# Attention and a gated convolution in one kernel: whole-unit copies of the transposed probabilities, more extra products at the start, and another order table

## The chip, the cores and the metric

The kernel runs on one core of one Trainium2 chip. The metric is the device time of one execution in microseconds (us). A core has five instruction streams that run side by side and wait for one another through semaphores: PE (TensorE: matrix products, with the loading of weights shown apart as PEld), DVE (VectorE), ACT (ScalarE), POOL (GpSimd) and SP, whose queue (SPq) issues all the loads and stores here. Each stream works through its own list in order.

## The reference

q, k and v have 4 batches, 8 heads, 768 rows and 64 columns. Every row attends to its neighbours within 15 positions and, beside them, to one summary of each block of 32 rows (the elementwise maximum of k, the mean of v). The result, 768 x 512 a batch, goes through a gated layer.

```python
k_sum = k.reshape(B, H, nb, 32, D).max(axis=3)
v_sum = v.reshape(B, H, nb, 32, D).mean(axis=3)
scores_l = np.where(abs(i - j) < 16, q @ k.T / 8, -1e9)
scores_s = q @ k_sum.T / 8 + log(32)
a = softmax(concat[scores_l, scores_s])
x = a @ concat[v, v_sum]                     # heads side by side: B, S, 512
gate = sigmoid(causal depthwise convolution of x, 5 taps)
out = (gate * (x @ w_val)) @ w_out
```

## The kernel before

The 768 rows of a batch are cut into three thirds of 256 rows, which gives 12 groups g (4 batches by 3). Each group has two units, u = 2g and 2g + 1, of four heads each: 24 units for the attention, 12 groups for the two products with w_val and w_out. A unit's scores are eight blocks of 128 rows by 120 columns (window, own block, block summaries).

The instructions are written in the order of a table of tokens, ORDER, and each engine keeps that order. A token is a letter and its indices; a helper op_<letter> issues its instructions. Those that the text speaks of:

- PE: S.u.r scores of half a unit (two halves a unit), T.u transposes of a unit's probabilities (16 products with the identity), X.u probabilities times v, V.g.c half of x times w_val, O.g.s half of the product with w_out, VB sums of v for batch 0, VS transposes of the block sums of later batches, pw.k extra products of zeros that nothing reads.
- DVE: ks block maxima of k, N.u.c adds the mask and finds the row minimum, R.u reciprocal of the row sums, A.u.k one of the eight taps of the convolution on half a unit, gf gate times value, and the bit work on the weights (wvd, wve for w_val; wod, woe for w_out).
- ACT: E.u.c exponentials, C copies the transposed probabilities from PSUM to SBUF, H and F copy a unit's x out of PSUM (rounded and exact), I.u.r first tap, G.u gate, gh rounds gf, oe takes the output out of PSUM, wvs and wos rescale the weights, vb copies the block means of batch 0.
- POOL: mset fills the tile that pw reads, kc writes the maxima between the columns of k, M.u.r scales half a unit's probabilities, L and gl the low parts of x and of gf, tr sums blocks of v, wvc, wvb, woc and wob the high and low parts of the weights.
- SP: k, n, q, q0, v, w, o, m, c, i load; f.g.e.h copies the block means into v's tiles; st stores.

In group 0 V and O are single-pass float32 products; the others are split into 24 and 12 products of high and low parts. V.0 needs all four quarters of w_val; the four quarters of w_out are unpacked into the same tile wf, so woe.k can't begin before V.0.0 and V.0.1 are done with quarter k, and O.0 needs all of them.

PSUM has eight banks. psum_plan gives them out in two rings: two slots of two banks for the scores of a unit or its transposed probabilities (s), and four single banks for all else (p). A slot goes to the next tile once the last reader of the one before it has run. The tables of loads have two tiles each for q, k (by pair of heads) and v, so a load of v for group g + 2 waits for X of group g.

C.u.e in this kernel copies half e of a unit's 2 x 8 x 64 transposed probabilities, 512 columns of 120 partitions, so a unit has C.u.0 and C.u.1. Each pw token is two products of 128 x 64 by 104 columns; there are six of them, all into one bank.

Of the kernel before, what the change touches and what calls it, by code (L numbers as in the profile page):

```python
# [58 lines left out]
N.3.0 R.2 E.3.1 E.3.0 q.2 S.5.1 S.5.0 E.3.3 wve.1 E.3.2 N.5.0 M.2.1 N.5.3 N.5.2 N.5.1 S.4.1 wvc.1
S.4.0 n.0.1 VB.1 M.1.0 T.1 vb.0 vb.1 C.1.0 E.5.0 R.3 N.4.3 v.0.1 v.0.0 w.3 wvs.3 X.0 I.0.1 F.0 I.0.0  # L60
N.4.1 wvd.3 N.4.0 N.4.2 wve.3 w.2 wvd.2 C.1.1 M.3.0 wvc.0.1 v.1.1 X.1 v.1.0 A.0.0 A.0.1 A.0.2 M.3.1
A.0.3 k.1.3 wvb.0 M.2.0 T.2 wvs.2 E.5.1 wve.2 I.1.1 F.1 A.0.4 I.1.0 A.1.0 A.0.5 wvb.1 k.1.0 h.1
wvc.2.1 A.1.1 A.0.6 ks.1.3 kc.1.3 T.3 C.3.0 V.0.0 C.2.1 E.5.2 C.2.0 wvc.3.1 A.0.7 k.1.1 ks.1.1
kc.1.1 ks.1.0 wvb.3 kc.1.0 E.5.3 R.5 E.4.3 M.5.1 q.3 S.6.1 E.4.2 n.1.1 E.4.0 A.1.2 M.5.0 pw.5 G.0
N.6.3 gf.0.0 A.1.3 E.4.1 N.6.2 A.1.4 R.4 f.1.0.1 f.1.1.0 f.1.1.1 f.1.0.0 X.2 C.3.1 H.2 k.1.2 M.4.0
X.3 F.2 F.3 I.2.0 H.3 ks.1.2 I.3.0 S.6.0 N.6.0 N.6.1 v.2.1 T.5 C.5.1 C.5.0 A.1.5 v.2.0 A.3.0 A.2.0
I.3.1 S.7.1 A.1.6 A.3.1 A.1.7 A.3.2 kc.1.2 S.7.0 N.7.0 A.3.3 o.1 E.6.0 E.6.2 n.1.0 q.4 N.7.3 A.3.4
N.7.2 A.3.5 M.4.1 T.4 E.6.3 C.4.0 G.1 C.4.1 I.2.1 E.7.3 E.7.0 N.7.1 A.3.6 V.0.1 wod.1 tr.1.1 S.9.0
tr.1.0 gf.0.1 o.0 A.3.7 A.2.1 wod.0 A.2.2 wos.0 wos.1 woe.0 woe.1 G.3 f.2.0.0 f.2.0.1 o.2 E.7.2
S.8.1 wvb.2 L.3 wod.2 S.8.0 S.9.1 f.2.1.0 f.2.1.1 o.3 X.5 wod.3 wos.2 woe.2 h.2 L.2 woc.1.1 wos.3  # L70
woe.3 n.1.3 tr.1.3.1 F.5 E.6.1 H.5 E.7.1 X.4 F.4 H.4 woc.2 O.0.1 oe.0.1 O.0.0 A.2.3 R.6 M.6.0 A.2.4
N.9.0 M.6.1 A.2.5 N.8.3 A.2.6 R.7 A.2.7 I.5.0 G.2 I.5.1 I.4.0 N.8.1 N.8.0 N.9.1 n.1.2 tr.1.2 N.8.2
A.4.0 woc.0 v.3.0 k.2.2 k.2.3 N.9.2 A.4.1 A.5.0 v.4.1 E.8.0 n.2.0 oe.0.0 q.5 A.4.2 A.5.1 v.3.1 E.8.2
V.1.1 N.9.3 VS.1 A.5.2 gf.1.1 E.8.3 I.4.1 vs.1 T.6 L.4 M.7.0 M.7.1 T.7 C.6.1 wob.0 E.9.1 v.4.0 C.7.1
ks.2.3 kc.2.3 A.5.3 k.2.1 A.4.3 C.7.0 L.5 woc.3.1 wob.3 gh.1.1 A.5.4 f.3.1.0 f.3.0.0 f.3.0.1 wob.2
# [630 lines left out]
```

## Time and profile before

| | us |
|---|---|
| median of three timed runs | 241.03 (240.19 to 242.12) |
| profiled execution, whole | 242.98 |
| its span, first to last instruction | 241.2 |
| PE busy | 221.4 (92%) |
| ACT busy | 186.4 (77%) |
| DVE busy | 171.4 (71%) |
| POOL busy | 155.8 (65%) |

Busy times are unions over the span, and a matmul's end is modelled, so PE's share says that something was in it and not that it ran at its best. The span is what the rows below are read against; the profiled execution as a whole is 1.8 us longer.

### The profile page before, as it was taken

Reading aid. Unit: us, or ns where it says so; the run is one execution under the profiler, and the core shown is the slowest. Engines: PE = TensorE matmul, PEld = TensorE weight load, DVE = VectorE, ACT = ScalarE, POOL = GpSimd, SP = SyncE. Lnnn points to the kernel's source line nnn. Section 1 sums busy time; section 2 is a strip of 40 time slices with the busy share of each in tenths; the row PEclk is TensorE's granted clock in tenths of the full one; section 3 lists DMA queues with packets and bytes.
Section 4 is the critical chain, followed back from the end, with each engine's and each line's share of the span. In section 5 each row is a group of like instructions: output and inputs, shape, how many; then the busy total and the mean of one; then the engine's idle time right before and its main releaser. Section 6 shows DMA issues by size and latency. Waiting matters only on the chain.

```text
span 241.2 us, 7772 instructions
## 1 busy us (share of the span) xinstructions
PE 221.4 (92%) x2884; PEld 187.3 (78%) x2884; DVE 171.4 (71%) x683; ACT 186.4 (77%) x614; POOL 155.8 (65%) x219
## 2 busy tenths in 40 slices
...
GB/s 188 398 357 293 393 369 292 335 327 331 168 267 155 366 281 260 292 109 247 293 91 238 63 154 296 74 140 69 91 226 72 46 63 45 43 46 43 0 46 132
DMA packets 17318, 46.42 MB, mean 192 GB/s; under 512 B 2400, under 2 KB 3424, under 8 KB 17280
## 3 DMA queue, kind: packets, MB, share of 16 engines
...
q8 instruction: 23, 0.38, 0.6%
q14 instruction: 15, 0.12, 0.2%
...
## 4 chain that ended last, share of the span: by engine, by line
PE 71%; POOL 9%; DVE 6%; DMA 5%; ACT 4%; issue 3%; SPq 1%; POOLq 0%; ACTq 0%; DVEq 0%
PE val L567 26%; PE out L596 23%; PE x L513 9%; PE s L444 7%; POOL p L487 4%; PE pt L496 4%; DMA v<-vb 2%; DVE sn L460 2%; POOL vT L326 2%; DMA k<-in_kT_dram 1%; DVE wf L409 1%; POOL xl L533 1%; POOL gl L581 1%; DVE g L547 1%; ACT g L542 1%
## 5 line engine op out<-in xcount | busy, mean ns | idle before, releaser
L547 DVE SCALAR_TENSOR_TENSOR g<-xf,cwt,g 128x256 f32<-128x256 f32 x192 | 88.4, 483 | 12.4 <-ACT g L542 8.8
L474 ACT ACTIVATE p<-sn,nm 128x120 f32<-128x120 f32 x192 | 73.9, 397 | 5.9 <-DVE nm L460 3.0
L487 POOL TENSOR_TENSOR p<-p,ri 128x480 f32<-128x480 f32 x48 | 47.3, 1001 | 22.5 <-DVE ri L482 18.3
L460 DVE CUSTOM_DVE_ANT_0 sn<-s,mask 128x120 f32<-128x120 f32 x192 | 42.4, 276 | 14.7 <-PE s L444 14.3
L567 PE MATMUL val<-xh,wv 128*128 128x256 f32 x352 | 50.1, 284 | 0.0
L567 PEld LDWEIGHTS val<-xh,wv 128*128 128x128 f32 x352 | 45.3, 188 | 1.9 <-issue 0.6
L596 PE MATMUL out<-wo,gh 128*128 128x512 f32 x176 | 45.6, 401 | 0.0
L581 POOL TENSOR_TENSOR gl<-gf,gh 128x512 fp32r<-128x512 f32 x22 | 28.4, 1294 | 19.8 <-ACT gh L576 18.7
L474 ACT ACTIVATION_READ_ACCUMULATOR p<-sn,nm 128x1 f32 x192 | 38.5, 201 | 0.0
L596 PEld LDWEIGHTS out<-wo,gh 128*128 128x128 f32 x176 | 31.8, 188 | 7.4 <-ACT g L542 0.4
L533 POOL TENSOR_TENSOR xl<-xf,xh 128x512 fp32r<-128x512 f32 x22 | 28.4, 1295 | 9.2 <-ACT xf L528 6.6
L444 PE MATMUL s<-k,qbd 64*64 64x120 f32 x768 | 25.3, 279 | 6.8 <-POOL k L315 3.5
L444 PEld LDWEIGHTS s<-k,qbd 64*64 64x64 f32 x768 | 21.1, 140 | 11.0 <-POOL k L315 6.3
L326 POOL TENSOR_TENSOR vT<-vT 128x384 f32<-128x384 f32 (+3 forms) x48 | 27.2, 566 | 2.8
L513 PE MATMUL x<-pts,v 120*64 120x64 f32 x768 | 27.2, 224 | 1.9 <-DMA v<-vb 1.2
L513 PEld LDWEIGHTS x<-pts,v 120*64 120x64 f32 x768 | 25.3, 138 | 3.9 <-issue 1.8
L567 PE MATMUL val<-xl,wv 128*128 128x256 f32 x176 | 27.8, 279 | 0.0
L500 ACT COPY pts<-pt 120x512 f32<-120x512 f32 x48 | 26.7, 592 | 1.4 <-PE pt L496 1.3
L572 DVE SCALAR_TENSOR_TENSOR gf<-gt,val 128x512 f32<-128x512 f32 x24 | 16.4, 685 | 13.2 <-PE val L567 12.8
L596 PE MATMUL out<-wo,gl 128*128 128x512 f32 x88 | 24.3, 396 | 0.2 <-POOL gl L581 0.2
L567 PEld LDWEIGHTS val<-xl,wv 128*128 128x128 f32 x176 | 23.8, 188 | 0.0
L606 ACT ACTIVATE ob<-out 128x512 f32<-128x512 f32 x23 | 13.8, 599 | 11.6 <-PE out L596 7.6
...
## 6 DMA issues: line engine op xcount, KB each, us to landing
...
```

Of the source, the lines that this page charges most:

```text
L326: nc.gpsimd.tensor_tensor(dst, src[:, :, :n], src[:, :, n : 2 * n], ALU.add)
L444: nc.tensor.matmul(sp[64 * e : 64 * e + 64, h, c * KW : c * KW + KW], qbd[g % NQB][64 * h : 64 * h + 64, pr, i * QT : i * QT + QT], ktile( ...
L460: nc.vector.tensor_tensor_reduce(sn[:, n, :], tiles["s", u][:, h, c * KW : c * KW + KW], mask[:, mv, :], -1.0 / math.sqrt(D), 3.0e38, ALU.add,
L474: nc.scalar.activation(p[:, n, :], tiles["sn", u][:, n, :], AF.Exp, bias=tiles["nm", u][:, n : n + 1], scale=-1.0, accum_out=rs[:, u % NRS ...
L487: nc.gpsimd.tensor_tensor(p[:, w], p[:, w], ri[:, w].unsqueeze(2).broadcast_to([P, TPU, KW]), ALU.mult)
L500: nc.scalar.copy(pts[:, :, QT * e : QT * e + QT], tiles["pt", u][:KW, e])
L513: nc.tensor.matmul(dst, v[:KW, i, c0 : c0 + D], src, start=True, stop=g > 0)
L533: nc.gpsimd.tensor_tensor(xl[:, prs(u), :], xf(g)[:, prs(u), HALO:], tiles["xh", g][:, prs(u), :].bitcast(F32), ALU.subtract,)
L547: nc.vector.scalar_tensor_tensor(gt, xf(u // NHP)[:, pr, o : o + SG], cwt[:, pr, o : o + 1], gt, ALU.mult, ALU.add)
L567: nc.tensor.matmul(val[:, r], w, x, start=(n == 0), stop=(n == len(terms) - 1))
L581: nc.gpsimd.tensor_tensor(gl[:, cos, :], tiles["gf", g, cp], tiles["gh", g][:, cos, :].bitcast(F32), ALU.subtract)
L596: nc.tensor.matmul(po, x, w, start=(n == 0), stop=(n == len(terms) - 1))
```

## The change

Four things change. C.u is one copy of both halves, 1,024 columns over the two banks of the slot, in place of two of 512. There are twelve pw tokens, each with a PSUM tile of its own; the first has twelve products and the others two. The bank plan follows from that. And the table ORDER is another one: the same tokens otherwise, in another order on every engine. Two of the table's rows stand for it here.

```diff
-NWARM = 2
+NWARM = (12,) + (2,) * 11

 ORDER = """
-k.0.1 mset pw.0 q0.1 ks.0.1 k.0.0 ks.0.0 kc.0.1 S.0.1 pw.1 pw.2 kc.0.0 c cs q0.0 m N.0.3 E.0.3 N.0.2
...
+n.0.2 k.0.2 ks.0.2 q0.2 mset pw.6 pw.0 VB.2 pw.5 k.0.3 pw.2 pw.10 pw.1 kc.0.2 S.1.0 c q0.3 cd ks.0.3
...
-        return {"vb": [("vb", a[0])], "VS": [("vsp", a[0])], "vs": [("vsp", a[0])], "pw": [("pw", 0)]}.get(
+        return {"vb": [("vb", a[0])], "VS": [("vsp", a[0])], "vs": [("vsp", a[0])], "pw": [("pw", a[0])]}.get(
...
-        for j in range(NWARM):
+        for j in range(NWARM[k]):
...
-                ps(("pw", 0), [P, DM])[:QT, : QT + BASE], t[:, :QT], t[:, : QT + BASE],
+                ps(("pw", k), [P, DM])[:QT, : QT + BASE], t[:, :QT], t[:, : QT + BASE],
...
-    def op_C(u, e):
+    def op_C(u):
         pts = wt(("pts", u), [KW, NP, P], "pts")
-        nc.scalar.copy(pts[:, :, QT * e : QT * e + QT], tiles["pt", u][:KW, e])
+        nc.scalar.copy(pts.rearrange("p n (e q) -> p e n q", e=2), tiles["pt", u][:KW])
```

Three places show how instructions move. The lines of the changed kernel are two lower, since its table is two lines shorter. In a name the last number is a running count; before it stands, for k, the pair of heads.

PE at the start of the program, before (pw extra products, s scores, vb sums of v):

```order
L332 MATMUL pw_87<-ones 64x104 x2
L444 MATMUL s_99<-k_1_78,qbd_69 64x120 x8
L332 MATMUL pw_87<-ones 64x104 x4
L444 MATMUL s_99<-k_0_93,qbd_69 64x120 x8
L444 MATMUL s_148<-k_0_93,qbd_70 64x120 x8
L444 MATMUL s_148<-k_1_78,qbd_70 64x120 x8
L344 MATMUL vb_176<-vn_174,ones 64x512
L344 MATMUL vb_178<-vn_174,ones 64x512
L332 MATMUL pw_87<-ones 64x104 x2
```

PE at the start, now:

```order
L330 MATMUL pw_92<-ones 64x104 x2
L330 MATMUL pw_95<-ones 64x104 x12
L342 MATMUL vb_108<-vn_78,ones 64x512
L342 MATMUL vb_110<-vn_78,ones 64x512
L330 MATMUL pw_112<-ones 64x104 x2
L330 MATMUL pw_117<-ones 64x104 x2
L330 MATMUL pw_120<-ones 64x104 x2
L330 MATMUL pw_123<-ones 64x104 x2
L442 MATMUL s_128<-k_2_80,qbd_69 64x120 x8
L442 MATMUL s_128<-k_3_115,qbd_69 64x120 x8
```

The first scores now come from heads 2 and 3 (unit 1), and 20 extra products and a VB stand ahead of them, where two extra products stood before.

PE from V.0.0 (val_0 from xf and wf, the float32 product of group 0) on, before:

```order
L567 MATMUL val_0_590<-xf_241,wf 128x256 x8
L444 MATMUL s_627<-k_1_606,qbd_70 64x120 x8
L332 MATMUL pw_87<-ones 64x104 x2
L513 MATMUL x_667<-pts_599,v_485 64x64 x16
L513 MATMUL x_690<-pts_588,v_485 64x64 x16
L444 MATMUL s_627<-k_0_560,qbd_70 64x120 x8
L496 MATMUL pt_730<-ident,p_417 120x64 x16
L444 MATMUL s_755<-k_3_526,qbd_70 64x120 x8
L444 MATMUL s_755<-k_2_687,qbd_70 64x120 x8
L496 MATMUL pt_800<-ident,p_622 120x64 x16
L567 MATMUL val_1_832<-xf_241,wf 128x256 x8
```

PE from T.2 on, now:

```order
L494 MATMUL pt_581<-ident,p_360 120x64 x16
L330 MATMUL pw_598<-ones 64x104 x2
L565 MATMUL val_0_614<-xf_227,wf 128x256 x8
L565 MATMUL val_1_623<-xf_227,wf 128x256 x8
L494 MATMUL pt_641<-ident,p_213 120x64 x16
L494 MATMUL pt_668<-ident,p_465 120x64 x16
L511 MATMUL x_730<-pts_609,v_602 64x64 x16
L511 MATMUL x_749<-pts_747,v_602 64x64 x16
L442 MATMUL s_781<-k_1_658,qbd_70 64x120 x8
L442 MATMUL s_781<-k_0_726,qbd_70 64x120 x8
L442 MATMUL s_833<-k_3_358,qbd_70 64x120 x8
L442 MATMUL s_833<-k_2_558,qbd_70 64x120 x8
```

V.0.1 (val_1) has moved from behind X.2, X.3 and the scores of units 6 and 7 to right behind V.0.0, with T.3 and T.4 behind it and ahead of X.2.

DVE around the first block maxima of batch 1 (ks_3 from k_3, the token ks.1.3), before:

```order
L409 SCALAR_TENSOR_TENSOR wf<-sc_wv_547,wf 128x512
L547 SCALAR_TENSOR_TENSOR g_467<-xf_241,cwt,g_467 128x256
L547 SCALAR_TENSOR_TENSOR g_552<-xf_241,cwt,g_552 128x256
L547 SCALAR_TENSOR_TENSOR g_467<-xf_241,cwt,g_467 128x256
L547 SCALAR_TENSOR_TENSOR g_552<-xf_241,cwt,g_552 128x256
L547 SCALAR_TENSOR_TENSOR g_467<-xf_241,cwt,g_467 128x256
L302 TENSOR_REDUCE ks_3_567<-k_3_526 128x24
L547 SCALAR_TENSOR_TENSOR g_467<-xf_241,cwt,g_467 128x256
L302 TENSOR_REDUCE ks_1_608<-k_1_606 128x24
L302 TENSOR_REDUCE ks_0_612<-k_0_560 128x24
L481 TENSOR_REDUCE ri_619<-rs 128x8
L482 RECIPROCAL ri_619<-ri_619 128x8
```

DVE around ks.1.3, now:

```order
L407 SCALAR_TENSOR_TENSOR wf<-sc_wv_246,wf 128x512
L479 TENSOR_REDUCE ri_345<-rs 128x8
L480 RECIPROCAL ri_345<-ri_345 128x8
L458 ISA sn_332,nm_333<-s_273,mask 128x120
L458 ISA nm_333 128x1
L458 ISA sn_332,nm_333<-s_273,mask 128x120
L458 ISA nm_333 128x1
L398 TENSOR_SCALAR wf<-raw_wv_354 128x512
L300 TENSOR_REDUCE ks_3_378<-k_3_358 128x24
L407 SCALAR_TENSOR_TENSOR cwt<-sc_cw_164,cwt 128x20
L458 ISA sn_332,nm_333<-s_273,mask 128x120
L458 ISA nm_333 128x1
```

ks.1.3 stood behind most taps (g) of units 0 and 1; now it stands ahead of the last mask additions (sn) of unit 2, and so ahead of all taps.

## Rows read from the trace of the kernel before

**Rows 1.** Busy time by stage: us and instructions of PE, PEld, DVE, ACT, POOL; clock, DMA, GB/s.

```profile
0.00:73.70 73.70, 59.03 (x852) 43.53 (x852) 59.36 (x254) 59.34 (x210) 47.49 (x81) 0.98 0.86 305
...
73.70:237.10 163.40, 162.32 (x2033) 143.78 (x2032) 112.03 (x430) 126.48 (x404) 108.34 (x138) 1.00 0.44 144
```

**Rows 2.** Chain of waits, kinds of TensorE work later in the run.

```profile
73.79 1.80 PE s L444 x64
...
75.59 2.02 PE x L513 x64
...
148.88 0.43 PE vsp L360 x4
...
165.90 1.08 PE pt L496 x32
...
182.44 2.83 PE val L567 x24
...
225.95 8.40 PE out L596 x36
```

**Rows 3.** TensorE in order of time, first 65 us.

```profile
5.92 1.08 PE L444 MATMUL s<-k,qbd 64*64 64x120 f32 x16 [3.46 <-POOL k L315]
...
6.93 1.65 PE L332 MATMUL pw<-ones 128*64 128x104 f32 x8
...
14.91 1.06 PE L444 MATMUL s<-k,qbd 64*64 64x120 f32 x32
...
20.76 1.94 PE L344 MATMUL vb<-vn,ones 128*64 128x512 f32 x8
...
33.19 3.72 PE L567 MATMUL val<-xf,wf 128*128 128x256 f32 x16 [0.38 <-ACT g L542]
...
48.42 5.41 PE L567 MATMUL val<-xf,wf 128*128 128x256 f32 x16
...
57.58 7.13 PE L596 MATMUL out<-wf,gf 128*128 128x512 f32 x16
```

**Rows 4.** Chain of waits: its head by line, and one piece of it.

```profile
by line: PE val L567 26.3%; PE out L596 23.0%; PE x L513 8.5%; PE s L444 7.3%; POOL p L487 4.0%; PE pt L496 4.0%; issue 2.9%; DMA v<-vb 2.4%; DVE sn L460 2.1%; POOL vT L326 1.9%; DMA k<-in_kT_dram 1.5%; DVE wf L409 1.1%; POOL xl L533 1.1%; 
...
34.88 5.78 DMA v<-vb
```

**Rows 5.** Busy time of shorter early stretches, columns as in rows 1.

```profile
0.00:9.00 9.00, 3.80 (x32) 2.88 (x36) 2.81 (x10) 2.36 (x7) 1.70 (x14) 1.00 0.79 256
...
9.00:17.00 8.00, 7.01 (x113) 4.64 (x115) 5.12 (x32) 6.45 (x34) 1.24 (x6) 1.00 1.04 398
...
17.00:21.00 4.00, 3.47 (x46) 2.00 (x40) 3.92 (x24) 3.36 (x14) 1.64 (x2) 1.00 0.74 240
```

**Rows 6.** The same view, two later stretches.

```profile
49.40:52.60 3.20, 3.20 (x10) 2.50 (x9) 1.28 (x8) 3.20 (x13) 2.75 (x4) 0.51 0.96 296
...
60.00:112.00 52.00, 49.67 (x689) 42.01 (x689) 45.04 (x198) 48.30 (x163) 49.88 (x73) 1.00 0.71 236
```

**Rows 7.** Groups by line: three of POOL, two ACT copies out of PSUM.

```profile
L487 POOL TENSOR_TENSOR p<-p,ri 128x480 f32<-128x480 f32 x48 | 47.3, 1001 | 22.5 <-DVE ri L482 18.3 <-ACT ob L606 1.8 <-ACT p L474 1.5
...
L500 ACT COPY pts<-pt 120x512 f32<-120x512 f32 x48 | 26.7, 592 | 1.4 <-PE pt L496 1.3
...
L533 POOL TENSOR_TENSOR xl<-xf,xh 128x512 fp32r<-128x512 f32 x22 | 28.4, 1295 | 9.2 <-ACT xf L528 6.6 <-ACT xh L525 2.6
...
L326 POOL TENSOR_TENSOR vT<-vT 128x384 f32<-128x384 f32 (+3 forms) x48 | 27.2, 566 | 2.8
...
L603 ACT ACTIVATE ob<-out 128x256 f32<-128x256 f32 x1 | 0.4, 386 | 2.2 <-PE out L596 2.2
```

**Rows 8.** VectorE in order of time: its first mask addition.

```profile
7.81 0.28 DVE L460 CUSTOM_DVE_ANT_0 sn<-s,mask 128x120 f32<-128x120 f32 x1
```

**Rows 9.** All engines in order of time, the end.

```profile
236.04 1.10 PE L596 MATMUL out<-wo,gl 128*128 128x512 f32 x4
...
237.68 0.60 ACT L606 ACTIVATE ob<-out 128x512 f32<-128x512 f32 x1 [2.87 <-DMA out_dram<-ob]
```

More of the change, by code (lines that the diff above doesn't have):

```diff
@@ L59 @@
[L59 to L75, printed above, removed]
@@ new lines @@
+VB.4 k.0.0 pw.7 pw.8 N.3.0 E.3.0 N.1.1 ks.0.0 pw.3 n.0.0 VB.0 h.0 E.3.2 N.3.3 k.0.1 ks.0.1 E.1.1
+E.3.1 E.3.3 w.0 wvd.0 wvs.0 R.1 kc.0.0 q0.0 S.0.0 kc.0.1 S.0.1 S.2.1 n.0.5 S.2.0 N.0.3 n.0.1 n.0.3
+E.0.3 N.0.0 M.1.0 N.0.1 R.3 N.0.2 VB.5 i M.1.1 T.1 M.3.0 N.2.2 N.2.3 wve.0 E.0.1 E.0.0 E.0.2 R.0
+N.2.1 M.0.1 M.0.0 w.2 w.1 n.1.1 k.1.3 E.2.3 tr.1.1 VB.3 VB.1 C.1 E.2.1 wvd.1 ks.1.3 ce N.2.0 wvs.1
+wvs.2 wvd.2 pw.9 T.0 wvc.0.1 wve.2 kc.1.3 wvc.2.1 vb.0 vb.1 q.2 S.4.1 C.0 wve.1 S.4.0 N.4.1 E.2.2
+N.4.2 N.4.0 E.2.0 R.2 M.2.1 N.4.3 S.5.0 E.4.1 S.5.1 N.5.3 N.5.0 wvc.1 E.4.3 v.0.1 v.0.0 X.1 I.1.1
@@ new lines @@
+kc.2.3 wob.0 I.6.0 n.2.1 q.6 X.7 I.7.0 H.7 R.8 gf.2.0 N.10.3 N.10.1 N.11.2 st.0.0 n.2.0 F.7 A.6.0
+N.11.1 N.11.3 N.10.2 I.7.1 E.10.2 M.8.1 O.1.0 oe.1.0 f.4.1.0 M.8.0 O.1.1 M.9.0 kc.2.1 M.9.1 T.9
+N.11.0 T.8 L.6 h.4 A.6.1 A.6.2 gl.2.1 A.6.3 E.10.0 q.7 f.4.0.1 v.5.0 f.4.1.1 E.10.1 gh.2.0 k.3.0
+v.5.1 A.7.0 ks.2.2 A.7.1 A.7.2 A.6.4 E.10.3 L.7 V.3.1 E.11.2 C.8 E.11.1 C.9 gl.2.0 kc.2.2 S.13.0
+ks.2.0 kc.2.0 S.12.0 oe.1.1 E.11.0 E.11.3 A.7.3 A.6.5 R.10 M.10.0 M.10.1 S.13.1 A.6.6 A.7.4 A.7.5
+k.3.2 st.1.0 A.6.7 G.6 tr.2.0 S.12.1 f.4.0.0 X.8 A.7.6 A.7.7 G.7 N.13.3 N.13.1 E.13.1 X.9 H.8 F.8
@@ new lines @@
+N.14.3 N.14.2 F.11 A.10.0 N.14.0 N.15.2 A.10.1 A.10.2 I.11.0 n.3.2 N.15.0 gf.4.0 A.10.3 M.13.1
+A.11.0 A.11.1 N.15.1 N.15.3 E.14.1 gh.3.1 gl.3.1 E.14.0 L.10 M.13.0 V.4.1 A.10.4 gf.4.1 st.2.0
+f.7.1.1 A.11.2 st.2.1 f.6.0.1 f.6.1.0 E.14.3 gh.4.0 gh.4.1 A.11.3 A.11.4 A.11.5 E.14.2 R.14 ks.3.2
+A.10.5 A.10.6 O.3.0 T.13 C.13 A.11.6 A.11.7 A.10.7 h.6 tr.3.0 T.12 gl.4.1 L.11 C.12 E.15.0 E.15.1
+E.15.3 O.3.1 gl.4.0 S.16.1 f.7.0.1 S.17.0 S.16.0 N.16.0 oe.3.1 kc.3.0 G.11 E.15.2 S.17.1 N.16.3 G.10
+ks.3.3 M.14.1 N.17.3 f.6.0.0 N.16.2 oe.3.0 N.17.1 E.16.0 f.6.1.1 X.12 H.12 R.15 M.15.0 I.12.1 I.12.0
```

109 lines of the change are left out of this document (53 added, 56 removed).

## Prediction

> **What bounds the kernel now.** I read the busy times by stage first [rows 1]. From 73.7 us to 237.1 TensorE is busy for 162.3 of 163.4 us at the full clock; before 73.7 it is busy for 59.0, and part of that at half pace. So the second part is bound by TensorE's list, and what can be won lies in the first 73.7 us or in the list itself. To see how much, I price TensorE's list by its pieces at the full clock [rows 2]: a half of S 0.45 us (64 records, two units, 1.80), X 1.01, T 0.54, a half of V 2.83, a half of O 2.80, VS 0.43. Group 0 [rows 3]: V.0 3.5 a half (16 records in 3.72, less the tail of the last), O.0 3.5 (16 in 7.13), VB 0.95 (8 records in 1.94), X.0 and X.1, which have twice the products, 1.87. An extra product takes 0.2 us at half pace (8 records in 1.65 are four products: 0.4 each), and 0.1 a record at full pace.
>
> Up to the end of V.1.0 the old list holds 20 S, 6 VB, 8 T, 6 X, four halves of group 0, two of V.1, one VS and six pw: 48.1 us. V.1.0 ended at 73.8 (the S of [rows 2] follow it). So TensorE had **lost 25.7 us** by then. The whole list is 206.6 us and ended at 237.1 [rows 9]: 30.5 lost, so only 4.8 came after, most of it pieces a little dearer than my prices. Behind the last product come 4.1 us of copying and storing [rows 9].
>
> **The copies.** 24 copies of 1,024 columns take the place of 48 of 512 at 0.592 [rows 7]. Nearest rows: 256 columns took 0.386, so 256 more cost 0.206, and 1,024 would take 1.00, against two at 0.59 that overlap by about 0.1 when they follow one another. Bounds: 0.59 (the second bank is free) and 1.18 (it costs a full copy), so for a unit from 0.5 less to 0.1 more; I take nothing, as the slope's 1.00 is within 0.1 of the pair. ACT is not the bound after 73.7 (126.5 of 163.4), X now waits for one copy and not two. The sum doesn't hang on it.
>
> **The extra products.** 34 instead of 12. Twenty of the new ones and a VB stand ahead of the first score, and the queue of TensorE holds the score behind them. 14 products at half pace from 1.5 us on end at 7.1, VB (twice 0.95) at 9.0, 8 more at 12.2; if the clock rises after the first dozen, the first score starts at 8.7. The price is not the difference to 5.9, where the first score started [rows 3]: the mask now stands behind q.1 in the load order, 2.23 MB from the start, which is 9 to 10 us at 256 GB/s [rows 5], and the first mask addition (7.81 before [rows 8]) waits for it. Two halves of S must be through by then, at 1.08 each at half pace: 14.4 against 9.7 us. So the block costs 0 at the one end, 4.7 us at the other. Which: 16 score records at 5.92 took 1.08, 32 at 14.91 took 1.06, so the pace was 1.2 GHz until about 14, though TensorE had hardly paused from 5.9 on; the granted clock reads 1.00 there and doesn't show it. I take 1 us; the wait of ks.1.3 for its load, below, swallows it, so nothing of it enters the sum. In the Trainium skill, "TensorE: Matmul & The Clock Gate", Part 1, sustained activity releases a throttle that is the default, and the ramp is put at under 1% of a typical span, which would make the block worth less than 2.4 us either way. The trace agrees that the start is slow, and shows it lasting longer than one would read there.
>
> **The new order, TensorE's list to V.1.0.** The same count with 6 T, no VS and 8 more pw is 48.8. I follow what each piece waits for, with loads placed by their bytes in the new order. 5.5 MB were in by 17 us and 398 GB/s flowed from 9 us on; then the rate fell to 240 [rows 5], because q.2 had to wait for unit 1's scores, which came late. In the new order these scores come early and q.2 follows k.1.3, so I let the rate go on at 390 to 400.
> - DVE: the eight mask additions of units 1 and 3 run from about 9.7 without the gaps of before, then units 0 and 2. ks.1.3 stands at the head of its queue from about 21 and its load (7.3 MB) lands at about 22: 1 us or 2 lost, with the last addition of unit 2 behind it.
> - X.1 needs v.0 (8.9 MB: 26) and the copy C.0 (26): X.1 and X.0 take 26.7 to 30.4.
> - V.0.0 needs the fourth quarter of w_val (10.3 MB: 30, then rescaled and joined) and F.0: 32.3. V.0.1 follows at once, until 39.4. Before, V.0.1 started at 48.4 and took 5.4 [rows 3], as the clock had fallen to 0.51 from 49.4 to 52.6 [rows 6].
> - T.3, T.4, then X.2 at 40.6. X.2 waits for f.1, which landed at 40.7 before, after 5.8 us on the way [rows 4]. Now two loads of v.2 stand ahead of it, and these wait for X.0 (30.4); four issues of f end at 36, landing 38 to 41. So X.2 is no earlier than before, but V.0.1 and T.4 lie behind it already.
> - X.3, four S until 44.4, X.4 at 45.5. O.0.1 waits for the four quarters of w_out, unpacked one by one on ACT and DVE after X.3's copies: 48.2, so it ends at 49.5. T.5 50.0, O.0.0 53.5, X.5 54.5, four S 56.3, V.1.1 59.1, V.1.0 62.0. Before: O.0 from 57.6 on.
>
> That is 62.0 - 48.8 = 13.2 lost instead of 25.7.
>
> **Who is late next.** POOL. It worked 47.5 of the first 73.7 us, so it had lost 26.2, and 49.9 of the 52 us from 60 to 112 [rows 1, 6]: TensorE's lead can't be larger than POOL allows. The piece that decides is V.3.1, whose last products need L.7. Ahead of L.7 POOL's new list has 20 M at 0.96, 9 L and gl at 1.28, 5 tr at 2.5 [rows 7] and 22 us of weight parts and small copies: 65.4, and TensorE's list to the end of V.3.1 has 69.3. V.3.1 ends 1.7 after L.7. So TensorE's loss there is POOL's loss less 2.2. Counted as above (M.7.1, with 44.2 ahead of it, done at 61.8), POOL loses 17.6.
>
> The end follows: list 208.8 (206.6 and 22 more products at 0.1), loss at V.3.1, 4.3 for dearer pieces behind it (26.3 to 30.5 before), 4.1 of tail, so **span = 217.2 + loss at V.3.1**. POOL's counted 17.6 is a lower bound, since counting leaves out waits that the profile puts to nothing; "issue" has 2.9% of the chain [rows 4], 7.0 us. I add a third of that, 2.4, as a quarter of the span with most of the load traffic lies in question. POOL's loss 20.0, TensorE's 17.8, span 235.0. The profiled span of 241.2 stands to the median of 241.03 as -0.2, so I predict **234.8 us**.
>
> **The rivals.**
> 1. Everything goes as counted: loss 15.4, 232.4 us. For it: after 73.7 TensorE waited for nothing that cost much. Against it: before, waits without a name did occur.
> 2. POOL comes no earlier than before. ks.1.3 on DVE and tr.1.1 on POOL stand at the head of their queues before the units 2 to 5 are through, and each us that their loads land late holds all M behind them; M.11.1 now has 79.5 of POOL work ahead of it instead of 68.8. With POOL's loss at 26.2 to 26.8, TensorE's is 24 to 24.6, and the time 241.0 to 241.6: no change.
> 3. Slower: the clock. In the new list TensorE waits in small pieces between 44 and 50 (the w_out quarters, T.5 for M.5.1), as it did before the fall at 49.4 [rows 6]. If it falls there and stays at the low level through O.0, X.5 and the scores into V.1, these run at twice their price: 3.5 + 3.5 + 1.0 + 1.8 = 9.8 us, 244.6. It decides once the low level lasts some 17 us; before, it lasted 3.2.
> 4. That the change doesn't do what it says is out: the order shows one copy a unit and the twelve series.
>
> **How the numbers follow.** A measurement of this kernel tells about 1% from no change (2.4 us). Chances: forecast (232.5 to 238.5) 0.53, rival 1 with what lies below 232.5 0.16, rival 2 and the stretch up to 243.4 0.19, slower 0.12. Faster 0.69, same 0.19, slower 0.12. The range must leave out no more than 0.2: it takes in rival 1 and rival 2, 230.5 to 241.8.
>
> **What would show it.** Right: V.0.1 right behind V.0.0 before 41 us; O.0 ended before 56; V.1.0 ended at 62 to 66; POOL's idle time up to M.7.1 17 to 21 us; TensorE full from there on; one copy of about 1.0 us a unit. Wrong: the first score later than 11; f.1 landing after 44; ks.1.3 waiting more than 3 us; stretches of low clock between 40 and 60; gaps on TensorE behind 75 us, above all at V.3.1 and T.11.

## The result and the profile after

The changed kernel took **243.49 us** (median of 16, 241.69 to 246.60) beside 240.98 for the kernel before (16 runs, 238.22 to 242.81): ratio **1.0122**, 95% interval 1.0087 to 1.0157, so slower by 1.2%. The forecast was 234.8, and 243.49 lies above the whole range. (Ratios leave disturbed executions out, so they are not quite the quotient of the medians.) The profiled execution took 245.63 with a span of 243.9.

Busy time by stage of the changed kernel, cut where [rows 1] is cut (columns as there):

```profile
0.00:73.70 73.70, 62.93 (x876) 47.82 (x876) 56.29 (x240) 53.40 (x183) 46.13 (x79) 0.91 0.86 313
73.70:240.00 166.30, 164.23 (x2060) 144.18 (x2056) 117.02 (x444) 131.55 (x407) 109.59 (x141) 1.00 0.44 137
```

Behind 73.7 us TensorE is again busy nearly throughout (2.1 us idle). The first stage has a mean clock of 0.91 where it had 0.98, and its last piece, V.1.0, ends at 72.9 where 62.0 was forecast: against the forecast, that is where to look. Beside the kernel before (73.7) V.1.0 is no later, but two T and the VS, which stood ahead of it, now stand behind it. TensorE in this stage, in order of time (start, us, pieces, idle before and its releaser); the pieces of [rows 3] are among them:

```profile
8.62 2.23 PE L442 MATMUL s<-k,qbd 64*64 64x120 f32 x64
...
17.23 3.48 PE L442 MATMUL s<-k,qbd 64*64 64x120 f32 x64 [3.09 <-DVE wf L398]
...
29.24 1.26 PE L442 MATMUL s<-k,qbd 64*64 64x120 f32 x32 [1.96 <-ACT pts L498]
...
35.67 0.69 PE L494 MATMUL pt<-ident,p 64*120 64x64 f32 x16
...
37.01 7.14 PE L565 MATMUL val<-xf,wf 128*128 128x256 f32 x32
...
50.65 1.12 PE L594 MATMUL out<-wf,gf 128*128 128x512 f32 x2
52.10 1.13 PE L594 MATMUL out<-wf,gf 128*128 128x512 f32 x2 [0.33 <-DVE wf L407]
54.45 1.12 PE L594 MATMUL out<-wf,gf 128*128 128x512 f32 x2 [1.22 <-DVE wf L407]
57.53 2.07 PE L594 MATMUL out<-wf,gf 128*128 128x512 f32 x2 [1.96 <-DVE wf L407]
59.53 1.11 PE L494 MATMUL pt<-ident,p 64*120 64x64 f32 x16
...
72.82 0.60 PE L358 MATMUL vsp<-ident,vsT 128*24 128x128 f32 x4
```

The first score starts at 8.62, as counted. V.0.1 does follow V.0.0 at once: 32 records from 37.01 in 7.14. But X.0 ends at 35.6 (T.2 starts at 35.67), V.0.1 at 44.1, O.0.1, which takes its four quarters one at a time, at 59.5, and V.1.0, ahead of the VS, at 72.9, where 30.4, 39.4, 49.5 and 62.0 were forecast. Two steps hold nearly all of it: **5.2 us late by X.0, 4.8 more by the end of O.0.1**; 0.9 come after.

The clock in that stage, by stretches (columns as above):

```profile
14.00:16.00 2.00, 0.14 (x2) 0.00 (x0) 1.16 (x5) 2.00 (x12) 0.84 (x4) 1.00 1.03 381
...
18.00:20.00 2.00, 2.00 (x48) 2.00 (x44) 0.84 (x9) 0.51 (x3) 1.56 (x2) 0.50 1.02 403
...
30.00:34.00 4.00, 4.00 (x87) 3.70 (x81) 3.24 (x24) 2.82 (x14) 3.06 (x4) 0.58 0.73 289
...
57.00:61.00 4.00, 3.47 (x19) 1.74 (x20) 3.93 (x19) 1.18 (x5) 3.15 (x7) 0.57 0.34 136
```

Behind each pause (14 to 17 us, 27 to 29, 53 to 57) comes a stretch at 1.2 GHz (mean granted clock 0.50 to 0.58), in which S took 3.48 us instead of 1.87. SP's queue in order of time, up to w_out's last quarters:

```profile
25.44 0.33 SPq L269 DMA_DIRECT2D k<-in_kT_dram  x1
35.73 0.81 SPq L281 DMA_DIRECT2D v<-in_vw_dram  x2
36.71 0.98 SPq L371 DMA_DIRECT2D v<-vb  x1
37.75 0.47 SPq L287 DMA_DIRECT2D raw_wo<-in_wo_dram  x1
...
46.92 0.98 SPq L287 DMA_DIRECT2D raw_wo<-in_wo_dram  x2
```

SP stands still from 25.4 to 35.7 behind v.2, which waits for X.0; the first quarter of w_out follows at 37.75, the last two at 46.92. The copy itself, by lines (count, busy us, mean ns, idle before), beside the two of 592 in [rows 7]:

```profile
L498 ACT COPY pts<-pt 120x1024 f32<-120x1024 f32 x24 | 23.9, 1007 | 4.0 <-PE pt L494 3.8
```

1.007 us: the estimate of 1.00 was right. The end, to set beside [rows 9]:

```profile
240.34 0.60 ACT L604 ACTIVATE ob<-out 128x512 f32<-128x512 f32 x1 [1.88 <-PE out L594]
```

From V.1.0 to this last copy of an output it is 167.4 us, where the forecast had room for 168.9. So the rear came out close to the forecast in sum, and the forecast failed in front of V.1.0.

### The profile page after: what moved, and what is told of

It reads as the page before. It is cut to its first block, busy times and chain, and to the rows that moved or that the text cites. A ratio compares the mean times of both kernels' runs of the same rounds, so it can differ in the third digit from the quotient of the medians.

```text
span 243.9 us, 7832 instructions
## 1 busy us (share of the span) xinstructions
PE 227.5 (93%) x2928; PEld 192.0 (79%) x2928; DVE 173.3 (71%) x683; ACT 185.5 (76%) x590; POOL 155.7 (64%) x219
## 4 chain that ended last, share of the span: by engine, by line
PE 43%; ACT 20%; DMA 12%; issue 9%; POOL 5%; DVE 4%; SPq 4%; ACTq 0%; DVEq 0%; POOLq 0%
PE out L594 17%; PE val L565 14%; ACT p L472 8%; PE x L511 5%; PE s L442 3%; DMA raw_wv<-in_wv_dram 3%; ACT pts L498 3%; DMA v<-in_vw_dram 3%; DMA raw_wo<-in_wo_dram 3%; PE pt L494 3%; DMA k<-in_kT_dram 2%; ACT g L540 2%; POOL gl L579 2%; SPq L371 2%; POOL p L485 2%
## 5 line engine op out<-in xcount | busy, mean ns | idle before, releaser
L545 DVE SCALAR_TENSOR_TENSOR g<-xf,cwt,g 128x256 f32<-128x256 f32 x192 | 87.4, 485 | 16.9 <-ACT g L540 12.7
L565 PE MATMUL val<-xh,wv 128*128 128x256 f32 x352 | 49.6, 283 | 0.2 <-DVE gf L570 0.2
L565 PEld LDWEIGHTS val<-xh,wv 128*128 128x128 f32 x352 | 44.4, 188 | 1.9 <-issue 0.5
L472 ACT ACTIVATION_READ_ACCUMULATOR p<-sn,nm 128x1 f32 x192 | 37.2, 194 | 0.0
L511 PEld LDWEIGHTS x<-pts,v 120*64 120x64 f32 x768 | 26.6, 140 | 5.6 <-issue 3.1
L511 PE MATMUL x<-pts,v 120*64 120x64 f32 x768 | 29.0, 227 | 1.8 <-ACT p L472 0.8
L324 POOL TENSOR_TENSOR vT<-vT 128x384 f32<-128x384 f32 (+3 forms) x48 | 27.8, 578 | 3.0
L442 PE MATMUL s<-k,qbd 64*64 64x120 f32 x768 | 24.8, 280 | 5.2 <-DVE wf L398 3.1
L498 ACT COPY pts<-pt 120x1024 f32<-120x1024 f32 x24 | 23.9, 1007 | 4.0 <-PE pt L494 3.8
L540 ACT ACTIVATE g<-x,cwt 128x256 f32<-128x256 f32 x40 | 18.2, 455 | 3.1 <-PE x L513 1.2
```

The lines of the kernel that those rows point to most:

```text
L324: nc.gpsimd.tensor_tensor(dst, src[:, :, :n], src[:, :, n : 2 * n], ALU.add)
L442: nc.tensor.matmul(sp[64 * e : 64 * e + 64, h, c * KW : c * KW + KW], qbd[g % NQB][64 * h : 64 * h + 64, pr, i * QT : i * QT + QT], ktile( ...
L472: nc.scalar.activation(p[:, n, :], tiles["sn", u][:, n, :], AF.Exp, bias=tiles["nm", u][:, n : n + 1], scale=-1.0, accum_out=rs[:, u % NRS ...
L498: nc.scalar.copy(pts.rearrange("p n (e q) -> p e n q", e=2), tiles["pt", u][:KW])
L511: nc.tensor.matmul(dst, v[:KW, i, c0 : c0 + D], src, start=True, stop=g > 0)
L545: nc.vector.scalar_tensor_tensor(gt, xf(u // NHP)[:, pr, o : o + SG], cwt[:, pr, o : o + 1], gt, ALU.mult, ALU.add)
```

## The experiments

Each was timed beside the kernel before on one chip, whose median there was 240.1 to 240.5. The places in the list of the profiled execution, in us (X.0 by the start of T.2, V.1.0 by the start of what follows it), and the timed executions:

| | X.0 | O.0.1 | V.1.0 | last copy | median (runs) | ratio to before, 95% |
|---|---|---|---|---|---|---|
| forecast | 30.4 | 49.5 | 62.0 | 230.9 | 234.8 | |
| changed kernel | 35.7 | 59.5 | 72.8 | 240.3 | 243.49 (16) | 1.0122 [1.0087, 1.0157] |
| e0, the same again | 34.5 | 57.9 | 70.8 | 238.5 | 244.08 (6) | |
| b0, the kernel before again | | | 70.9 | 234.9 | 240.18 (1) | |
| e6, q0 ahead of w_val | 34.4 | 58.3 | 72.9 | 241.7 | 246.13 (6) | 1.0270 [1.0204, 1.0336] |
| e8, w_out in the gap | 32.1 | 58.7 | 71.8 | 239.7 | 243.49 (6) | 1.0150 [1.0085, 1.0215] |
| e11, products fitted | 34.6 | 59.1 | 73.9 | 242.2 | 244.95 (6) | 1.0196 [1.0130, 1.0262] |
| e13, loads rearranged | 32.6 | 53.8 | 66.6 | 234.2 | 241.27 (12) | 1.0030 [0.9990, 1.0070] |
| e14, both | 33.9 | 53.6 | 66.4 | 237.3 | 241.78 (12) | 1.0067 [1.0026, 1.0109] |
| e16, e13 and more | 32.9 | 54.0 | 66.8 | 234.6 | 240.39 (12) | 0.9985 [0.9941, 1.0030] |

**Which of the three parts it is.** First the kernel unaltered (e0):

> The changed kernel unaltered, for a second profile and as the measure for the next three. Theory (the order's places cost it: loads that stand at the head of SP's queue, and pauses of TensorE behind which the granted clock falls): 242 to 244 us as before, with TensorE idle between 14 and 17 us and SP's queue standing still from 25 to about 35 us again. Rival (the profile was a chance one): the pauses are gone or elsewhere, and V.1.0 ends more than 3 us earlier than 73.

244.08 (240.11 to 245.80): the pauses and SP's standstill are there again (SP waits 6.5 us for X.0), with shorter falls of the clock and none behind the pauses in O.0 (1.00 from 57 to 61 us). V.1.0 ends 2 us earlier than in the first profile, so the rival falls too. The whole copy alone, at the place of the second half (e1; the tokens of unit 1 stand for those of all units):

```diff
-T.1 vb.0 vb.1 C.1.0 E.5.0
+T.1 vb.0 vb.1 E.5.0
...
-wvd.2 C.1.1 M.3.0
+wvd.2 C.1 M.3.0
```

> The kernel before with the whole-unit copy alone: the old order, six pw of two products. Theory (the copy is neutral, the order is what costs): within 0.4% of before, 240 to 242 us. Rival A (the copy costs, since a unit's transposed probabilities reach X some 0.4 us later and ACT is held for 1.0 us in one piece): 242.5 to 244 us, the whole 2.5 us of the change.

243.02, ratio 1.0133 [1.0085, 1.0181]. **Rival A holds: the copy alone costs 2.6 us in the old order.** X.1 now stands and waits for it (TensorE, in order of time):

```profile
31.17 0.34 PE L511 MATMUL x<-pts,v 120*64 120x64 f32 x4 [2.40 <-ACT pts L498]
```

X takes its blocks in the order 0, 2, 1, 3, so its first half needs only the first half's columns; two copies let it begin on one. The halves, both at the place of the one copy, in the new order (e2; again unit 1 stands for all), and the new order with two products in the first pw (e3):

```diff
-VB.3 VB.1 C.1 E.2.1
+VB.3 VB.1 C.1.1 C.1.0 E.2.1
```

```diff
-NWARM = (12,) + (2,) * 11
+NWARM = (2,) * 12
```

> The changed kernel with two copies of 512 columns a unit, both at the place of the one. Theory: the time of the changed kernel, 242.5 to 244 us, within 1 us of the repeat, as two copies take 1.1 us together against 1.0. Rival A (the copy costs): 240 to 241.5 us.

> The changed kernel with two products in the first pw token, as in all others. Theory: the ten products bring little, as the mask is there only at 10 us and TensorE pauses at 14 anyway: 242.5 to 245 us, first score at about 7.6 us or at the arrival of its load. Rival B (the extra products cost their 1 to 2 us at the start): 241 to 242 us. Rival C (they raise the clock early and so earn much): 246 us or more, with the granted clock low until 14 us.

e2: 246.05, ratio 1.0174 [1.0106, 1.0243]; e3: 243.24, 1.0104 [1.0052, 1.0155]. In the new order halves at one place bring nothing back, and ten products more or less are not seen. e2, which has no whole copy, is slower than the kernel before too: the new order with its products and bank plan costs by itself. Halves at two places, as the old order has them, were not tried in it. Then, in the old order, the whole copy at the first half's place (e4: `T.1 vb.0 vb.1 C.1 E.5.0`), and with halves for units 0 to 5 and whole copies behind (e12):

> The kernel before with the whole-unit copy, now written where the first of the two halves stood and not where the second did. Theory D (the copy itself is neutral; what cost 2.6 us in the run with the copy at the second half's place is that X, which reads the first half's columns for its first 32 products, can no longer begin before the second place in ACT's list: C.1 began at 30.1 us there, its first half at 26.5 before): 240 to 241.2 us, C.1 at about 26.5 us. Rival A (1,024 columns in one piece cost their own price wherever they stand, by the E behind them that come 0.4 us later and the slot of the ring that is held longer): 242.5 to 243.5 us.

> The kernel before with halves for units 0 to 5 and the whole-unit copy, at the first half's place, for units 6 to 23. Theory D (the whole copy costs where X of the first groups starts on one half, as TensorE waits there; behind 73 us TensorE is full and it is neutral): within 0.3% of before, 239.5 to 241 us. Rival A (it costs everywhere, by the longer hold of the slot or of ACT): 241.5 to 242.5 us, as with all units whole at that place.

e4: 241.95, 1.0115 [1.0044, 1.0186]; e12: 242.19, 1.0089 [1.0049, 1.0128]. The place may be worth a part of the 2.6 us (the intervals overlap), but the price does not vanish with halves in the first six units: Theory D falls, and some 2 us stay with the copies behind them. So X.1's wait is one place of the price, not the whole; where the rest is lost is not shown.

**The kernel before again (b0).**

> The kernel before unaltered, for a second profile: its timed executions lie at 236 to 240 us of span, below the 241.2 of the one that the prediction was worked out from. Theory H (the prediction's baseline was a costly execution: the fall of the clock under V.0.1 at 49.4 us is not in most of them, so part of the loss of 25.7 that the new order was to win back was not there): span 236 to 240, V.1.0 ends at 69 to 72 us and not 73.8, V.0.1 takes 3.5 to 3.7 us and not 5.4. Rival: the same trace again, V.1.0 at 73 to 74.

Span 238.4, clock 0.999, V.1.0 ended at 70.9. TensorE in order of time: V.0.1, and the scores behind V.1.0:

```profile
45.60 3.72 PE L567 MATMUL val<-xf,wf 128*128 128x256 f32 x16
...
70.86 1.87 PE L444 MATMUL s<-k,qbd 64*64 64x120 f32 x64
```

V.0.1 takes 3.72 and not the 5.41 of [rows 3]: the low clock of [rows 6] is not in this execution. Nor is the stop that stood right ahead of it in the execution that was read, for which the profile names no releaser (the kernel before, first profile, TensorE in order of time):

```profile
47.93 0.56 PE L496 MATMUL pt<-ident,p 64*120 64x64 f32 x12 [1.74 <-issue]
```

Theory H holds: 2.9 of the 25.7 us "lost" belonged to the one execution that was read, and there was that much less to win.

**The two places, first attempts.** Of the order these cuts and those that follow show SP's tokens only. Moved on SP alone: f.1 and three quarters of w_out ahead of v.2 and of k.1.1 (e5); q0.0 and the identity ahead of w.0, whose bit work goes behind three of unit 2's four mask additions (e6); both (e7):

```diff
-v.1.0 v.1.1 k.1.1 v.2.0 v.2.1 f.1.0.0 o.0 f.1.0.1 f.1.1.0 f.1.1.1 k.1.0 q.3 o.1
+v.1.0 v.1.1 f.1.0.0 f.1.0.1 f.1.1.0 f.1.1.1 o.0 o.2 o.3 k.1.1 v.2.0 v.2.1 o.1 k.1.0 q.3
```

```diff
-k.0.1 w.0 q0.0 n.0.5 n.0.1 n.0.3 i
+k.0.1 q0.0 i n.0.5 n.0.1 n.0.3 w.0
```

> The changed kernel with the copies of the block means for group 1 (f.1) and the loads of the quarters 0, 2 and 3 of w_out issued ahead of the two loads of v.2, and quarter 1 right behind them, on SP alone. Theory (SP stands still behind v.2 until X.0 ends at about 35, and O.0 waits for the quarters that lie behind it): O.0.1 ends at 54 to 55 us instead of 59.5, V.1.0 4 to 5.5 us earlier than 73, the time 239 to 240.5 us. Rival E (the quarters wait for their bit work on ACT and DVE, not for their loads): O.0.1 within 1.5 us of 59.5, the time 242.5 to 244 us. Rival F (what is won at O.0 is lost again, POOL or later loads being the bound): O.0 early, but the time within 1 us of 243.5.

> The changed kernel with the last part of q for units 0 and 2 and the identity issued ahead of the first quarter of w_val, and that quarter's bit work behind the mask additions of unit 2. Theory (S.0 and R.1 waited for loads until 17.2 us, and the clock fell behind that pause): S.0.0 at 15 us instead of 17.2, the granted clock full from 14 to 25 us, X.0 ends 3 to 4.5 us earlier than 35.6, the time 239.5 to 241.5 us. Rival G (the start is bound by the bytes of all its loads): X.0 less than 1.5 us earlier, 242.5 to 244 us.

> The changed kernel with both of these moves. Theory: the two gains add, as the first lies ahead of X.0 and the second behind it: V.1.0 ends at 63 to 66 us, close to the 62 that was forecast, the time 235.5 to 238 us. Rival F (POOL or later loads bound the stretch from 62 to 112 us): V.1.0 early, but 239.5 us or more.

251.51, 246.13 and 250.61: all slower. In e5 VectorE's ks.1.1 stood at the head of its queue (VectorE, in order of time):

```profile
45.50 0.95 DVE L300 TENSOR_REDUCE ks<-k 128x24 f32<-128x768 f32 x1 [9.03 <-DMA k<-in_kT_dram]
```

Nine us for k.1.1, which I had put behind f.1. In e6 S.0 starts at 15.86, and yet S.4 no earlier than before (TensorE, in order of time):

```profile
15.86 1.87 PE L442 MATMUL s<-k,qbd 64*64 64x120 f32 x64 [1.37 <-DVE ri L479]
...
26.28 3.48 PE L442 MATMUL s<-k,qbd 64*64 64x120 f32 x64 [2.36 <-DVE nm L458]
```

S.4 waits for the last mask addition of unit 2. VectorE, for which the profile shows no wait for a load from 14 to 33 us, has the bit work of w.0, half of that of the next quarter and ks.1.3 ahead of it (VectorE, in order of time):

```profile
21.20 1.14 DVE L398 TENSOR_SCALAR wf<-raw_wv 128x512 uint32<-128x512 uint32 x1
22.44 1.28 DVE L407 SCALAR_TENSOR_TENSOR wf<-sc_wv,wf 128x512 uint32<-128x512 uint32 x1
23.64 1.23 DVE L398 TENSOR_SCALAR wf<-raw_wv 128x512 uint32<-128x512 uint32 x1
24.79 0.94 DVE L300 TENSOR_REDUCE ks<-k 128x24 f32<-128x768 f32 x1
```

TensorE stands, the clock falls there (0.50 from 26 to 30 us) and X.0 ends at 34.4. That is what Rival G had for X.0, and the loads did run at 388 to 413 GB/s from 14 to 32 us; but its reason, the bytes, is not what stops S.4 here, and 246.13 lies above its range.

**Gap and pauses.** e8 issues the quarters 0, 2 and 3 behind k.1.1; e9 puts 30 products into pw.3 and 2, 6 and 8 more ahead of T.0, S.4 and S.5; e10 does both. In e8 and e10 the low part of the last quarter of w_val is worked out after w_out's has taken its place in wf; the work is the same.

```diff
-k.1.1 v.2.0 v.2.1
+k.1.1 o.0 o.2 o.3 v.2.0 v.2.1
```

```diff
-NWARM = (12,) + (2,) * 11
+NWARM = (12, 2, 2, 30, 2, 2, 2, 2, 2, 4, 2, 2, 8, 6)
```

> The changed kernel with three of the four quarters of w_out issued right behind k.1.1, ahead of the loads of v.2, so that they are carried while the DMA engines have next to nothing to do (32.5 to 36.5 us), and unpacked in the order 0, 2, 3, 1. Nothing else is issued later. Theory (O.0 waits for quarters that queue behind other loads): O.0.1 ends at 53.5 to 55 us instead of 57.9 to 59.5, V.1.0 3 to 5 us earlier than in the repeat of the changed kernel, the time 239 to 241 us. Rival E (the bit work on DVE and ACT is what O.0 waits for): O.0.1 less than 1.5 us earlier, 242.5 to 244 us. Rival F (won there, lost behind): V.1.0 early, the time above 242.

> The changed kernel with 30 extra products where TensorE waits for the last part of q (pw.3) and 2, 6 and 8 more ahead of T.0, S.4 and S.5, where it waits again; nothing is moved. Theory (the clock falls behind these pauses and makes S, VB, T and X of the first 35 us cost twice): granted clock full from 12 to 36 us, X.0 ends 1 to 2.5 us earlier than 34.3, mean clock 0.99 or more, the time 241 to 242.5 us and with less spread. Rival G (the loads bound the first 32 us whatever the clock does): the clock is full, but X.0 ends within 0.7 us of 34.3, 243 to 244 us. Rival B (the products cost their own time): 244.5 us or more.

> Both of these: quarters of w_out in the gap and products in the pauses. Theory: the gains add, 237.5 to 239.5 us, V.1.0 at 66 to 68 us. Rival F (POOL or later loads bound the stretch behind): V.1.0 early, but 240.5 us or more.

e8: 243.49. Its list up to X.0 is the changed kernel's, but in its profiled execution the clock stayed full up to 50 us and X.0 ended at 32.1, not at 34.5 or 35.7: 2.4 to 3.6 us earlier, of which 0.4 to 0.5 lie ahead of S.0, and so ahead of the falls. Then k.1.0 was late (VectorE) and O.0 with it (TensorE); behind that wait the clock fell, and six records of O.0 took 5.49 us, where eight take 3.70 in e13 below. Nothing was won:

```profile
44.88 0.95 DVE L300 TENSOR_REDUCE ks<-k 128x24 f32<-128x768 f32 x1 [3.14 <-DMA k<-in_kT_dram]
```

```profile
53.30 5.49 PE L594 MATMUL out<-wf,gf 128*128 128x512 f32 x6 [2.85 <-DVE wf L407]
```

The clock there, by stretch (columns as above):

```profile
54.00:59.00 5.00, 5.00 (x12) 1.63 (x12) 4.93 (x23) 1.09 (x5) 5.00 (x6) 0.50 0.16 65
```

e9 (246.56, 1.0261) and e10 (244.85, 1.0220) tell little: a product took 0.19 us at the full clock, so 30 ended at 18.2 and held S.0 back by 2.2.

**Products to size, loads to size.** e11: VB.0 ahead of pw.3 with 13 products, 2, 4 and 4 more at the other places. e13: SP's list by the bytes that each consumer needs. e14: both.

```diff
-k.1.1 v.2.0 v.2.1 f.1.0.0 o.0 f.1.0.1 f.1.1.0 f.1.1.1 k.1.0 q.3 o.1 f.2.0.0 f.2.0.1 f.2.1.1 f.2.1.0 o.2 o.3
+k.1.1 k.1.0 o.0 o.2 f.1.0.0 f.1.0.1 f.1.1.0 f.1.1.1 v.2.0 v.2.1 q.3 o.1 o.3 f.2.0.0 f.2.0.1 f.2.1.1 f.2.1.0
```

> The changed kernel with the extra products cut to the pauses: VB.0 ahead of pw.3, which has 13 products (at 0.19 each, as the run with 30 showed, 2.4 us, from 14.5 to 17), and 2, 4 and 4 more ahead of T.0, S.4 and S.5. Theory K (the falls of the clock behind the pauses are what the changed kernel loses to the kernel before, whose executions have a mean clock of 0.996 to 1.0 against 0.97 to 0.99): mean clock 0.99 or more in most executions, X.0 ends at 32 to 33 us instead of 34.3 to 35.6, the time 240 to 241.5 us. Rival G (the clock follows and does not lead; the loads bound the start): clock full, but X.0 no earlier than 34 and the time 243 us or more.

> The changed kernel with SP's list from k.1.1 on in another order: k.1.0, quarters 0 and 2 of w_out, f.1, v.2, q.3, quarters 1 and 3, f.2; unpacked in the order 0, 2, 1, 3. In the run with three quarters in the gap k.1.0, f.1 and q.3 had become late instead (3.1, 1.8 and 0.6 us of waiting), so each of them now stands where its bytes fit. Theory (what O.0 and X.2 wait for is the order of the bytes, 400 per ns at most): X.2 at 42 to 43.5 us, no wait of DVE for k.1.0 over 1 us, O.0.1 ended by 54 to 56, V.1.0 at 68 to 70, the time 239.5 to 241.5. Rival E (ACT and DVE cannot have the quarters unpacked any earlier): O.0.1 at 57 us or later, 243 us or more.

> The rearranged loads and the fitted products together. Theory: the gains add, 237 to 239.5 us, below the kernel before (240.3). Rival F (the stretch behind V.1.0, POOL's list above all, takes what is won): V.1.0 at 67 or earlier, but 240.5 us or more.

**e13 did what was expected up to V.1.0:** 241.27, and 66.6 instead of 70.8 to 72.8. O.0 in one piece (TensorE, in order of time):

```profile
50.14 3.70 PE L594 MATMUL out<-wf,gf 128*128 128x512 f32 x8
53.77 0.68 PE L494 MATMUL pt<-ident,p 64*120 64x64 f32 x16
54.39 3.70 PE L594 MATMUL out<-wf,gf 128*128 128x512 f32 x8
```

Both causes of O.0's wait went with it. The quarters are there early, and their bit work falls where GpSimd has little to do. VectorE in e13, one of the two quarters that were unpacked with GpSimd idle:

```profile
47.26 0.42 DVE L398 TENSOR_SCALAR wf<-raw_wo 128x512 uint32<-128x512 uint32 x1
47.99 0.69 DVE L407 SCALAR_TENSOR_TENSOR wf<-sc_wo,wf 128x512 uint32<-128x512 uint32 x1
```

And in the changed kernel, the last quarter, VectorE and GpSimd's xl beside it:

```profile
54.32 1.49 DVE L398 TENSOR_SCALAR wf<-raw_wo 128x512 uint32<-128x512 uint32 x1
55.91 1.57 DVE L407 SCALAR_TENSOR_TENSOR wf<-sc_wo,wf 128x512 uint32<-128x512 uint32 x1
```

```profile
53.81 3.12 POOL L531 TENSOR_TENSOR xl<-xf,xh 128x512 fp32r<-128x512 f32 x2
```

Over four quarters the changed kernel's eight operations took 8.5 us, where four times 0.42 and 0.69 are 4.4 and e13 took 5.2. How much of the 4.8 is lateness of loads and how much this, e13 does not part.

e11 (244.95) and e14 (241.78) answer on the clock. e14's executions had a mean clock of 0.992 to 1.000, e13's 0.976 to 0.999, and e14 is no faster; e11's one execution with a mean clock of 1.000 took 244.15. Keeping the clock up with products did not pay. In the profiled executions of both, TensorE stopped at the same instruction, in the midst of X.0, without a releaser (e14):

```profile
33.55 0.28 PE L511 MATMUL x<-pts,v 120*64 120x64 f32 x2 [1.48 <-issue]
```

Theory K, that filling the pauses gives back what the falls cost, falls with them; what the products or these stops took back instead is not parted.

**A last step on the loads.** e15 takes q.3 ahead of o.0, v.2 ahead of f.1, and f.2 right behind o.1 and o.3; e16 also f.6 ahead of v.7.

```diff
-v.6.0 q.8 v.7.1 n.3.0 v.6.1 v.7.0 f.7.1.0
+v.6.0 v.6.1 q.8 f.6.0.1 f.6.1.0 f.6.0.0 f.6.1.1 v.7.1 n.3.0 v.7.0 f.7.1.0
```

> The kernel with rearranged loads, with q.3 moved ahead of quarters 0 and 2 of w_out, v.2 ahead of f.1, and f.2 right behind quarters 1 and 3. In the run before, S.6 waited 1.5 us for q.3, X.4 1.5 us for f.2, and the DMA engines were a third empty from 36 to 40 us behind f.1's small copies. Theory (up to O.0 the order of the bytes decides, and behind 73 us TensorE has no gaps of size, so that what is won at V.1.0 reaches the end): S.6 and X.4 without a wait over 0.5 us, V.1.0 at 63.5 to 65.5 us instead of 66.6, the time 238.5 to 240.5 us. Rival L (f.1 behind v.2 makes X.2 late by what the others gain): X.2 waits 1.5 us or more and V.1.0 is within 1 us of 66.6, 240.5 to 242 us.

> The same with v.6 in one piece and f.6 ahead of v.7, which waits for X.11. X.12 and X.13 waited 0.7 and 0.2 us for f.6 in the run before. Theory: these waits go, 0.5 to 1 us less than the run without it. Rival M (the waits behind 73 us are made up for elsewhere): within 0.5 us of it.

241.17 (1.0051 [1.0013, 1.0090]) and **240.39 (0.9985 [0.9941, 1.0030])**. In both X.2 waited for f.1 what S.6 and X.4 gained, which is Rival L. e16, TensorE in order of time:

```profile
44.52 2.12 PE L511 MATMUL x<-pts,v 120*64 120x64 f32 x64 [2.03 <-DMA v<-vb]
```

e16 is 0.8 below e15, as expected of f.6, but the intervals overlap, and in its profiled execution a wait of 1.57 stands at X.15 instead. It is 3 us better than the changed kernel and the same as the kernel before; nothing here beats that one.

## Why the prediction was wrong, by its own steps

- **"What bounds the kernel now": held.** TensorE is nearly full behind 73 us (2.1 us idle in the changed kernel); what e13 won at V.1.0 (4.2 against e0) reached the end (4.3).
- **"TensorE had lost 25.7 us by then": mis-sized.** One execution; the next one lost 70.9 - 48.1 = 22.8. The step "before, V.0.1 took 5.4, as the clock had fallen" counted as a gain what most executions had not lost: the mean clock of the kernel before over 85 executions is 0.997 (lowest 0.990), and 0.991 in the one read.
- **"The copies: I take nothing": wrong in the old order** (+0.9 to 1.3%), with the duration right. "X now waits for one copy and not two" overlooked that X began on one half, and that is only a part of the price (e12). No such price shows in the new order, where halves at one place were no faster.
- **"The extra products": right** within what e3 can tell. First score 8.62, first mask addition 10.10 (9.7). Its list, though, has a product at 0.1, the price of a record; a product is two records, 0.2 by its own row and 0.19 in e9, so at 0.19 the old list to V.1.0 is too short by 1.1 us and the new one by 3.1, and the losses too large by as much. The forecast does not move with it, as its V.3.1 was set by POOL. The losses below are by the prediction's list.
- **The failed step: the times of "X.1 and X.0 take 26.7 to 30.4" and of "unpack done 48.2".** Up to X.0 the loads did come nearly by their bytes, at 380 to 410 GB/s: w.0 at 16.7, where VectorE stood 1.6 us for it, with q0.0 behind it; after that the longest wait for a load is 0.5 us (ks.1.3, in e8). What the step left out is the clock: it prices every piece at full speed. With the clock full (e8) X.0 ended at 32.1, with falls at 34.5 and 35.7. Of the 5.2 us, 1.7 are there at the full clock too (X.1 starts at 27.8, and X.1 and X.0 take 4.3 and not 3.7); 3.5 are seen only with the falls, 0.5 of them ahead of S.0. For O.0 I priced the quarters by VectorE's undisturbed work, on loads that follow an X.0 at 30.4; they came from 44 us on, the bit work took twice its price, and O.0.1 ended at 59.5.
- **Rival 3, the clock, named what is seen, at other places, and had too small a chance.** I put the fall at 44 to 50; it came at 17 and 30, and in one profile at 57. The Trainium skill, "TensorE: Matmul & The Clock Gate", Part 1, puts the ramp at under 1% of a typical span, an estimate of less than 2.4 us here. These runs show more behind pauses: over 22 executions of the changed kernel the mean clock goes from 0.969 to 0.997 and the time with it, 1.5 us per 0.01 (correlation -0.84), with 6.5 us between the fastest and the slowest. That it is the cause of the whole difference is not shown: by the same line (an estimate) the changed kernel would need 241.8 at the 0.997 of the kernel before, whose mean is 240.2, and 241.3 at the full clock. So of 3.7 us between the means 1.6 remain that the clock does not go with.
- **"Who is late next: POOL": not reached, though rival 2's number was.** M.7.1 ended at 71.2 and not at 61.8, so POOL had lost 27.0, slightly more than rival 2 gave it for "no change", and V.3.1 ended at 94.4, a loss of 25.1 (rival 2: 24 to 24.6). But TensorE did not wait for POOL there: L.7 was done at 92.0 and the products that read it ran without a wait (POOL, then TensorE, in order of time).

```profile
69.26 3.83 POOL L485 TENSOR_TENSOR p<-p,ri 128x480 f32<-128x480 f32 x4
...
90.76 1.28 POOL L531 TENSOR_TENSOR xl<-xf,xh 128x512 fp32r<-128x512 f32 x1
```

```profile
93.83 0.63 PE L565 MATMUL val<-xl,wv 128*128 128x256 f32 x4
```

TensorE lost 1 us between V.1.0 and V.3.1, not 4.6; nearly all of its loss lies ahead of V.1.0.

- **The rear: right in sum (167.4 against 168.9), partly by luck.** The 1 us up to V.3.1 stands for 4.6, and 6.4 us of dearer pieces and waits behind it for 4.3. Against the kernel before it is 3.5 longer (164.0 in b0): two T and a VS that now stand behind V.1.0 are 1.5 of it, 1 is waiting, the rest dearer pieces. So an order that reaches V.1.0 4 us earlier (e13, e16) ends level, and one that reaches it no earlier is 3 us slower: e0 was at V.1.0 when b0 was (70.8 and 70.9) and lost 3.6 us behind it.

**Open:** why the clock falls behind a pause in one execution and not in the next, what stops X.0 in e11 and e14, where the whole copy costs the rest of its price, and what makes the pieces behind V.1.0 dearer.
